# An order of instructions found at build time by a clock per engine, and one transpose for both heads' last keys

## The chip, the cores and the metric

The kernel runs on one core of a Trainium2 chip. The metric is the device time of one execution in microseconds (us). TensorE (PE) multiplies, VectorE (DVE), ScalarE (ACT) and GpSimd (POOL) work elementwise or reduce, SyncE (SP) only issues transfers; each of the five runs its own instructions in the order in which they were issued to it, and waits on semaphores for the others.

## What is computed

Attention with a threshold, a Fourier mixing with a two-layer MLP, and a gated projection, one after the other:

```python
# attention: batch 4, heads 8, seq 576, head_dim 64
scores = scale * np.matmul(q, k.transpose(0, 1, 3, 2))
thresh = np.max(scores, axis=-1, keepdims=True) - tau
scores = np.where(scores >= thresh, scores, -1000000000.0)
attn = np.exp(scores - np.max(scores, axis=-1, keepdims=True))
attn = attn / (np.sum(attn, axis=-1, keepdims=True) + 1e-09)
x = np.matmul(attn, v)                      # then (B, S, H * D)
# Fourier mixing and MLP: d_model 512, hidden 2048
u = x + np.real(np.fft.fft(np.fft.fft(x, axis=1), axis=2))
un = (u - mu) / np.sqrt(var + 1e-06)
y = u + np.maximum(un @ w_ch1, 0.0) @ w_ch2
# gate: a causal convolution of 5 steps over y
out = (1.0 / (1.0 + np.exp(-gate_pre)) * (y @ w_val)) @ w_out
```

The weights arrive as 64-bit floats.

## The kernel before

**Attention** goes over 16 pairs of heads (4 batches of 4 pairs). A pair has 9 tiles: four of 128 queries for each head (h = 0 and 1), and one (h = 2) that holds the last 64 queries of both. For a tile, TensorE makes the scores (L539, two halves of 288 keys on the two halves of the array's rows), VectorE the negated maximum (L551), ScalarE the exponential (L558), VectorE the mask with the row sums (L568). ScalarE adds 1e-9 to the sums (L704), VectorE takes reciprocals (L672), GpSimd scales the tile (L575), and TensorE transposes its first 512 keys in four pieces (L609), which ScalarE copies out (L618). Scores have two PSUM buffers, so a tile's scores wait for the mask two tiles before. The last 64 keys of a head are the "tail": they are transposed apart (L589, 128 queries of one head at a time into 64 rows, on half the array's columns) and copied into th (L594), whose other 64 rows are zero (cleared in lines 172 to 174). Then the probabilities multiply v (L267, the two heads side by side on the two halves of the array's columns), once for the first 256 queries (c = 0) and once for the other 320, and ScalarE copies the result to xt (L270).

**Fourier stages.** A batch's four pairs are folded by GpSimd (L320 to L328) and run through 87 matmuls in two stages (L231), whose result GpSimd adds to x (L425 to L436) and SyncE stores as u_d.

**MLP.** The 2304 rows of u are cut in 5 chunks of 512, 384, 384, 512 and 512. In a chunk each of 16 hidden blocks takes 12 matmuls (h, L1045), a Relu (L1048), a split in high and low part (L1049) and 12 matmuls into four accumulators (c, L1061). **Weights** come as 32 pieces of 512 KB (raw, L852), which VectorE (L99, L100, L103, L104, L105), ScalarE (L101, L102, L108) and GpSimd (L109) turn into high and low float32 parts. The first 16 pieces may be stored in DRAM (e_h, e_l, L905) and reloaded (L835) since room for weights in SBUF opens in steps as attention's pools close: one of 16 blocks after the last keys, 8 when the last pair is folded, all when the last Fourier result is stored ("end" in on_mark, line 1165). Chunk 0's matmuls start when the score buffers are closed, and its last c block waits for "end". Then come the **gate** and the output (L1381, L1399).

**What sets the order.** Attention is a loop over steps of two tiles (line 656). In each step the pieces named in ORDER are issued one after the other:

```python
ORDER = 'R A1 F1 M0 N0 Q T0 M1 E0 E1 T1 U0 H1 TH P1 H3 A2 K0 F2 K1 C S2 S3 H2 WD WD N1 WP U1 WA P2'
```

M0, M1 are the maxima, E the exponentials, K the masks, C the sums, R the reciprocals of the step before, N its scaling, T the transposes of the tiles four behind (LAG), S2 and S3 the scores of the two tiles ahead. P1 and P2 issue tails, multiplications with v and Fourier matmuls from queues, up to a budget of ns (FILLS), and WD, WA, WP one operation each of the weights' conversion. After the last tile the letters of CYCLE do the same for the rest and chunk 0 (act(), line 1205). A transfer is issued where its piece of code stands; nearly all go through SyncE's queue.

## Time and profile before

| | us |
|---|---|
| median of 3 runs (lowest, highest) | 897.75 (897.50, 903.26) |
| the profiled execution, its own time | 897.85 |
| its span, first to last instruction | 896.1 |
| TensorE busy (4902 matmuls) | 837.1 |
| VectorE busy | 554.8 |
| ScalarE busy | 427.0 |
| GpSimd busy | 376.9 |

Busy time is the union of an engine's instructions over the whole span. The ends of matmuls are modelled, so two of them overlap by part of their length, and the distance between two starts says more than a duration. The stages have different limits; the rows further down are read by stretch. One matmul of the program with 32-bit operands shows as two in the profile, except the transposes.

### The profile page before, as it was taken

The numbers are of one execution on the slowest core, as the hardware profiler recorded it, in microseconds if no ns is written. First come the engines' busy times: TensorE is split into PE (matmuls) and PEld (weight loads), VectorE is DVE, ScalarE is ACT, GpSimd is POOL, SyncE is SP. The second block draws the span as 40 slices with busy tenths as digits, with TensorE's granted clock in tenths as the row PEclk, the third lists the DMA queues.
The fourth block names the chain that finished last, engine by engine and source line by source line (L and its number), as shares of the span: only waits on it lengthen the run. The fifth ranks groups of instructions, "written<-read, shape, count | busy, mean of one in ns | idle before, by whom it ended". The sixth has DMA issues, their size and how long they took to land.

```text
span 896.1 us, 13937 instructions
## 1 busy us (share of the span) xinstructions
PE 837.1 (93%) x4902; PEld 660.9 (74%) x4902; DVE 554.8 (62%) x1214; ACT 427.0 (48%) x854; POOL 376.9 (42%) x449
## 2 busy tenths in 40 slices
PE   6897899889997898999879999999999999999998
PEld 4554566546654665688669999999888888898896
DVE  7897987887989877257885443623122565527740
ACT  3776867667768575355453233232122232124432
POOL 3447855684599454443643132222010200056421
PEclk8999999999999899999989999999999999999999
DMA  7458237461592275772794044114000230253111
GB/s 190 118 146 246 67 110 235 141 191 41 166 318 71 71 235 177 245 251 89 255 361 171 18 165 130 71 60 128 2 1 0 101 100 1 99 183 107 60 41 65
DMA packets 63612, 117.10 MB, mean 131 GB/s; under 512 B 12466, under 2 KB 20530, under 8 KB 63544
## 3 DMA queue, kind: packets, MB, share of 16 engines
q1 hardware_dynamic: 56008, 92.36, 32.1%
q0 software_dynamic: 7104, 23.57, 8.1%
q8 instruction: 39, 0.64, 0.3%
q10 hardware_dynamic: 432, 0.30, 0.1%
q14 instruction: 29, 0.24, 0.1%
HBM read 84.73 MB, written 31.47 MB: 130 GB/s over the span
## 4 chain that ended last, share of the span: by engine, by line
PE 72%; DVE 14%; POOL 4%; DMA 4%; issue 3%; ACT 2%; SPq 1%; DVEq 0%; POOLq 0%; ACTq 0%
PE c L1061 20%; PE h L1045 19%; PE s L539 7%; PE f L267 6%; PE v L1381 5%; PE o L1399 5%; PE f L231 5%; PE t L609 4%; DVE p L568 4%; DVE neg L551 3%; POOL p L575 2%; DVE cx L103 1%; DVE raw L104 1%; PE f L589 1%; DMA qt<-in_q 1%
## 5 line engine op out<-in xcount | busy, mean ns | idle before, releaser
L1049 DVE SCALAR_TENSOR_TENSOR hl<-h,hh 128x512 fp32r<-128x512 f32 (+1 forms) x80 | 50.9, 636 | 186.0 <-ACT hh L1048 186.0
L1048 ACT ACTIVATE hh<-h 128x512 fp32r<-128x512 f32 (+1 forms) x80 | 44.3, 553 | 243.4 <-PE h L1045 243.3
L575 POOL TENSOR_SCALAR p<-p,su 128x576 f32<-128x576 f32 x144 | 111.3, 779 | 82.1 <-DVE su L672 74.7
L539 PE MATMUL s<-kt,qt 64*128 64x288 f32 (+1 forms) x640 | 101.2, 446 | 34.1 <-DVE p L568 29.3
L568 DVE SCALAR_TENSOR_TENSOR p<-s,thr,e 128x576 f32<-128x576 f32 x144 | 112.0, 815 | 19.6 <-ACT e L558 13.3
L1061 PE MATMUL c<-hl,w1h 128*128 128x512 f32 (+1 forms) x320 | 118.1, 369 | 0.1
L1061 PE MATMUL c<-hh,w1h 128*128 128x512 f32 (+1 forms) x320 | 118.1, 369 | 0.0
L1061 PE MATMUL c<-hh,w1l 128*128 128x512 f32 (+1 forms) x320 | 118.0, 369 | 0.0
L558 ACT ACTIVATE e<-s,neg 128x576 f32<-128x576 f32 x144 | 100.2, 738 | 36.2 <-DVE neg L551 36.0
L551 DVE TENSOR_REDUCE neg<-s 128x1 f32<-128x576 f32 x144 | 101.6, 746 | 15.7 <-PE s L539 15.6
L539 PEld LDWEIGHTS s<-kt,qt 64*128 64x128 f32 (+1 forms) x640 | 47.6, 179 | 76.2 <-issue 49.8
L609 PEld LDWEIGHTS t<-ident,p 128*128 128x128 f32 x576 | 63.5, 142 | 32.2 <-issue 15.4
L618 ACT ACTIVATE m<-t 128x512 f32<-128x512 f32 x144 | 84.3, 586 | 4.8 <-PE t L609 4.3
L609 PE MATMUL t<-ident,p 128*128 128x128 f32 x576 | 81.0, 282 | 5.4 <-POOL p L575 5.2
L1045 PE MATMUL h<-unh,w0h 128*128 128x512 f32 (+1 forms) x320 | 79.9, 371 | 3.8 <-ACT w0h L108 2.8
L1045 PE MATMUL h<-unh,w0l 128*128 128x512 f32 (+1 forms) x320 | 80.2, 372 | 2.7 <-POOL w0l L109 2.2
L1045 PE MATMUL h<-unl,w0h 128*128 128x512 f32 (+1 forms) x320 | 79.5, 370 | 0.0
L267 PE MATMUL f<-m,v 128*64 128x320 f32 (+1 forms) x512 | 72.5, 413 | 0.0
L1045 PEld LDWEIGHTS h<-unh,w0h 128*128 128x128 f32 x320 | 59.1, 189 | 12.0 <-ACT w0h L108 3.2
L1045 PEld LDWEIGHTS h<-unh,w0l 128*128 128x128 f32 x320 | 59.5, 191 | 11.3 <-POOL w0l L109 2.6
L1061 PEld LDWEIGHTS c<-hl,w1h 128*128 128x128 f32 x320 | 60.4, 189 | 8.5 <-DVE hl L1049 0.8
L1061 PEld LDWEIGHTS c<-hh,w1h 128*128 128x128 f32 x320 | 60.5, 189 | 7.9 <-issue 0.5
(232 smaller groups left out, 1427.0 us busy)
## 6 DMA issues: line engine op xcount, KB each, us to landing
raw<-in_moe_w_ch POOLq DMA_DIRECT2D x32, 512.0 KB, 5.7
qt<-in_q SPq DMA_DIRECT2D x30, 288.0 KB, 5.6
kt<-in_k SPq DMA_DIRECT2D x16, 288.0 KB, 4.8
ypad<-y_d SPq DMA_DIRECT2D x16, 288.0 KB, 3.8
out<-os SPq DMA_DIRECT2D x18, 256.0 KB, 2.0
v<-in_v SPq DMA_DIRECT2D x16, 256.0 KB, 2.7
e_h<-cx SPq DMA_DIRECT2D x16, 256.0 KB, 4.9
e_l<-ct SPq DMA_DIRECT2D x16, 256.0 KB, 3.5
```

Source lines behind the costliest of these rows:

```text
L231: PE.matmul(out=o, lhsT=l, rhs=r, start=(i == 0), stop=(i == n - 1))
L267: PE.matmul(out=f[h * 64:h * 64 + 64, 0:n], lhsT=w, rhs=r, start=(t == 0), stop=(t == 4))
L539: PE.matmul(out=s[o, c, 0:HALF], lhsT=qt[w, hh, q], rhs=kt[w, hh, :], start=True, stop=True)
L551: DVE.tensor_reduce(out=neg[i][:, j, 0:1], in_=sc[g][:, :, 0:HALF], axis=AX.XY, op=ALU.max, negate=True)
L558: ACT.activation(e, sc[g][:, :, 0:HALF], AF.Exp, bias=neg[g // 2][:, g % 2, 0:1], scale=1.0)
L568: DVE.scalar_tensor_tensor(out=p_view(g).rearrange("p (a b) -> p a b", a=2), in0=sc.pop(g)[:, :, 0:HALF], scalar=thr[g // 2][:, j], in1=ex ...
L575: POOL.tensor_scalar(out=v, in0=v, scalar1=su, scalar2=1.0, op0=ALU.mult, op1=ALU.mult)
L609: PE.matmul(out=f[:, t, :], lhsT=pv[:, t * 128:(t + 1) * 128], rhs=ident, is_transpose=True, start=(t == 0), stop=(t == 3))
L618: tq.append(lambda: ACT.activation(o, fv, AF.Copy))
L1045: PE.matmul(out=f[:, 0:n], lhsT=ww[:, k * 128:(k + 1) * 128], rhs=x[:, k, 0:n], start=(i == 0), stop=(i == 3 * KB - 1))
L1049: DVE.scalar_tensor_tensor(out=hl, in0=f[:, 0:n], scalar=0.0, in1=f32(hh), op0=ALU.max, op1=ALU.subtract)
L1061: PE.matmul(out=ch[c][o][:, 0:n], lhsT=ww[:, o * 128:(o + 1) * 128], rhs=x, start=(at_ == 0 and i == 0), stop=(at_ == FB - 1 and i == 2))
```

## The change

ORDER, CYCLE and the loop over steps are replaced by a class Loom. Each tile, tail, multiplication with v, Fourier transform, weight piece and block of chunk 0 is a generator. Before each instruction it yields the engine, an assumed length in ns, a rank and, for TensorE, the array's shape (row, col, full); between them it yields what it comes after. Loom keeps a clock per engine, adds a cost when TensorE's shape changes (SWITCH) and when an operation of VectorE and GpSimd would meet ("port"), and issues next the instruction with the earliest start, low ranks first. The order is fixed at build time; on the chip each engine still runs it in that order. Weight operations have rank 9, below all else, and Fourier matmuls are due one by one over 32 tiles (SPREAD). The convolution weights' conversion, one block of code before, becomes single operations of rank 9.

Beside it, the second head's keys are laid out so that its tail comes first (np.roll). One transpose of 128 x 128 turns both heads' last keys of a row block (L668); th holds head 0 in rows 0 to 63 and head 1 in rows 64 to 127, and vt is zero in the other half. For the 64 last queries two small matmuls do it (L672). kt gets a third copy of 288 columns for this (128x864): the second head's keys in their old order, for the last 64 queries. There are six buffers for probabilities, five before.

The diff, cut:

```diff
-ORDER = 'R A1 F1 M0 N0 Q T0 M1 E0 E1 T1 U0 H1 TH P1 H3 A2 K0 F2 K1 C S2 S3 H2 WD WD N1 WP U1 WA P2'
...
-PBUFS = 5
...
+PBUFS = 6
...
+SPREAD = 32
...
+RANK = {"D": 9, "A": 9, "P": 3}
...
+class Loom:
+    OVER = {"PE": 0.0, "DVE": 88.0, "ACT": 108.0, "POOL": 45.0}
+    SIGNAL = {"PE": 200.0, "DVE": 40.0, "ACT": 40.0, "POOL": 80.0}
+    SWITCH = {"full": 146.0, "row": 188.0, "col": 138.0}
...
+    def cost(self, t, s):
+        e, ns, rank, *how = t.want
+        if e == "PE" and self.shape not in how:
+            ns += self.SWITCH[how[0]]
+        if "port" in how:
+            ns += max(self.port["POOL" if e == "DVE" else "DVE"] - s, 0.0)
+        return ns
...
+    def pick(self, e):
+        c = [(self.start(t), t) for t in self.tasks if t.want[0] == e]
+        c = [x for x in c if x[0] is not None]
+        if not c:
+            return None
+        if e == "PE":
+            return min(c, key=lambda x: (self.score(*x), x[1].seq))
+        first = min(s for s, _ in c)
+        s, t = min((x for x in c if x[0] <= first + NEAR), key=lambda x: (self.rank(x[1]), x[0], x[1].seq))
+        late = s + self.cost(t, s) - HOLD[e]
+        if self.rank(t) >= 1:
+            better = [x for x in c if self.rank(x[1]) < 1 and x[0] < late]
+            if better:
+                s, t = min(better, key=lambda x: (x[0], self.rank(x[1])))
+        return s, t
+
+    def score(self, s, t):
+        r = self.rank(t)
+        v = s + (0.0 if self.shape in t.want else SWAP)
+        return v + 100.0 * r if r < 1 else v + FILL + 300.0 * (r - 1) - (STAY if t is self.last else 0.0)
...
-        ths = [[const.tile([128, 2, n], F32, name=f"th{i}_{n}") for n in (256, 320)] for i in range(2)]
-        for t in [vt for _, vt in vs] + ths[0] + ths[1]:
-            DVE.memset(t[64:128], 0.0)
+        ths = [[const.tile([128, n], F32, name=f"th{i}_{n}") for n in (256, 320)] for i in range(2)]
+        for _, vt in vs:
+            for h in range(2):
+                DVE.memset(vt[64 - h * 64:128 - h * 64, h], 0.0)
...
         def g_prep_qk(p):
+            if p >= 2:
+                yield "after", ("scored", p - 2)
             qt, kt = load_qk(p)
-            for _ in range(WAIT_QK):
-                yield
+            yield "delay", 7500.0
+            yield "POOL", 1060.0, 0.1, "port"
             POOL.tensor_scalar(out=kt, in0=kt, scalar1=alpha[:, 0:1], scalar2=1.0, op0=ALU.mult, op1=ALU.mult)
             kq[p] = (qt, kt)
-
-        def load_v(p):
+            loom.mark("kq", p)
...
             conv_w.load()
-            for _ in range(4):
-                yield
-            conv_w.convert()
-
+            yield "delay", 12000.0
+            for kind, op in conv_w.stages():
+                yield {"D": ("DVE", 170.0, 9), "A": ("ACT", 260.0, 9), "P": ("POOL", 222.0, 9)}[kind]
+                op()
...
+        def due(tile, least=1.0):
+            return lambda: max(2.0 + (tile - len(p_s)) / NPT, 1.0) if tile > len(p_s) else least
...
         def g_fft(b):
...
+            def rank():
+                done[0] += 1
+                r = due(NPT * (b + 1) + FFT_LATE + SPREAD * done[0] / FFT_OPS)
+                return (lambda: min(r(), END)) if b == B - 1 else r
...
-                    PE.matmul(out=s[o, c, 0:HALF], lhsT=qt[w, hh, q], rhs=kt[w, hh, :], start=True, stop=True)
+                    PE.matmul(out=s[o, c, 0:HALF], lhsT=qt[w, hh, q], rhs=kt[w, 2 if h == 2 and hh else hh], start=True, stop=True)
...
+        def g_sum(u):
+            yield "ACT", 203.0, 0.2
+            ACT.activation(ssum[u], ssum[u], AF.Copy, bias=1e-9)
+            yield "DVE", 155.0, 0.0
+            DVE.reciprocal(ssum[u], ssum[u])
+            loom.mark("r", u)
+
+        def g_tail(p, rows):
+            for j, i in enumerate(rows):
+                yield ("PE", 112.0 if i < 4 else 120.0, 0.4, "full" if i < 4 else "col", *(["room"] if j == 0 else []))
+                if j == 0:
+                    f, room = fill_tile()
+                x = p_t[p, i]
+                if i < 4:
+                    PE.transpose(f[:, j * 128:(j + 1) * 128], x[:, MAIN:MAIN + 2 * TAIL], ident)
+                else:
+                    for h in range(2):
+                        w = slice(h * 64, h * 64 + 64)
+                        PE.matmul(out=f[w, 0:64], lhsT=x[:, MAIN:S], rhs=ident[:, w], start=True, stop=True)
+            for i in rows:
+                loom.mark("tailed", p, i)
+            o, n = (256, 64) if rows[0] == 4 else (0, 256)
+            th = ths[p % 2][0 if rows[0] == 0 else 1]
+            yield "ACT", act(n), 0.3
+            ACT.activation(th[:, o:o + n], f[:, 0:n], AF.Copy)
+            loom.free(room)
+            loom.mark("th", p, rows[0])
...
+        def g_tile(g):
...
+            yield "after", ("kq", p), *([("s", g - 1)] if g else []), *([("k", g - 2)] if g > 1 else [])
+            yield "PE", 490.0 if h < 2 else 600.0, 0.1, "row"
+            emit_s(g)
+            loom.mark("s", g)
...
+            yield "DVE", 745.0, 0.3
...
+            yield "after", ("r", u), *([("n", g - 1)] if g else [])
+            yield "POOL", 737.0, 0.1, "port"
...
+            loom.mark("n", g)
+            yield "after", *([("t", g - 1)] if g else [("n", 0)]), *([("mc", g - 2)] if g > 1 else []), *([("pv", p - 2, c)] if p > 1 else [])
+            yield "PE", 437.0, 0.5, "full"
...
-            pv = p_view(g)
+            pv = v[:, TAIL if h == 1 else 0:]
...
-            if h == 1 and i % 2 == 1:
-                q_tail.append(g_tail(p, c, [p_t[p, i - 1 + j][:, hh * S + MAIN:hh * S + S] for hh in range(2) for j in range(2)], th[0:64, :, 0:256], (i - 1, i)))
-            if h == 2:
-                q_tail.append(g_tail(p, c, [p_t[p, i][:, MAIN:S]], th[0:64, :, 256:320], (i,)))
...
-        for u in range(NT // 2 + 3):
...
-            for atom in ORDER.split():
-                env[atom]()
...
+        def g_convert(k, raw, room):
             j, i = pieces[k][1]
-            stay = k >= EARLY and not isinstance(j, str)
-            if stay and j not in w:
-                return False
+            yield "delay", 8000.0
+            yield "when", lambda: at[0] == k and spare["cv"] and (k < EARLY or isinstance(j, str) or j in w)
...
+            took = {"D": iter((415.0, 415.0, 677.0, 679.0, 415.0)), "A": iter((715.0, 621.0, 635.0)), "P": iter((1035.0,))}
+            for kind, op in ops:
+                yield {"D": "DVE", "A": "ACT", "P": "POOL"}[kind], next(took[kind]), RANK[kind], "port"
+                op()
...
+            loom.add(g_load())
+            loom.add(g_first())
+            loom.run(lambda: heads[1] == FB)
...
-                    tick()
-                    slot("DAP", 4)
+                if c in (1, 2):
+                    loom.run(until=loom.now["PE"])
...
-    c["k"] = k.reshape(B, NP, 2, 2, HALF, D).transpose(0, 1, 3, 5, 2, 4).reshape(B, NP, 2 * D, 2, HALF)
+    k = np.stack([k[:, :, 0], np.roll(k[:, :, 1], TAIL, axis=-2), k[:, :, 1]], axis=2)
+    c["k"] = k.reshape(B, NP, 3, 2, HALF, D).transpose(0, 1, 3, 5, 2, 4).reshape(B, NP, 2 * D, 3, HALF)
```

On TensorE, in attention without a Fourier transform near: second half of the second pair, rows of before. s are scores, t transposes into the tile that m is copied from, f<-ident,p tails, f<-m and f<-th the multiplication with v.

```order
L539 MATMUL s<-kt,qt 128x288 x4
L609 MATMUL t<-ident,p 128x128 x8
L589 MATMUL f<-ident,p 64x128 x5
L539 MATMUL s<-kt,qt 128x288 x4
L609 MATMUL t<-ident,p 128x128 x8
L267 MATMUL f<-m_603,v_195 64x320 x8
L539 MATMUL s<-kt,qt 128x288 x4
L267 MATMUL f<-th_320_200,vt_196 64x320 x2
L609 MATMUL t<-ident,p 128x128 x8
L589 MATMUL f<-ident,p 64x128 x4
L539 MATMUL s<-kt,qt 64x288 x4
L539 MATMUL s<-kt,qt 128x288 x2
```

Here the transposes are those of tiles four to five behind the scores just ahead of them, and tails and multiplications with v stand where a budget let them in.

The same place after the change:

```order
L641 MATMUL s<-kt,qt 128x288 x4
L421 MATMUL f<-th_256_199,vt_196 64x256 x2
L739 MATMUL t<-ident,p 128x128 x8
L641 MATMUL s<-kt,qt 64x288 x4
L641 MATMUL s<-kt,qt 128x288 x2
L421 MATMUL f<-m_571,v_195 64x320 x6
L739 MATMUL t<-ident,p 128x128 x8
L668 MATMUL f<-ident,p 128x128 x2
L641 MATMUL s<-kt,qt 128x288 x4
L421 MATMUL f<-m_571,v_195 64x320 x2
L421 MATMUL f<-th_320_200,vt_196 64x320 x2
L739 MATMUL t<-ident,p 128x128 x8
```

A tail is two transposes of 128 rows in place of four of 64; the multiplication with v is cut in pieces (x6, x2) that stand directly behind scores; a step's transposes follow scores that are two tiles nearer than before.

On TensorE again, at the last Fourier transform, which runs beside chunk 0 (h and c are its blocks). Before, the second stage stands in pieces of 18, 9 and 18 matmuls between blocks; the last of them:

```order
L1045 MATMUL h<-unh,w0h_4643 128x512 x4
L1045 MATMUL h<-unh,w0l_4644 128x512 x4
L1045 MATMUL h<-unl,w0h_4643 128x512 x4
L231 MATMUL f<-csh,aeh 128x290 x3
L231 MATMUL f<-csh,ael 128x290 x3
L231 MATMUL f<-csl,aeh 128x290 x3
L231 MATMUL f<-ssh,boh 128x290 x3
L231 MATMUL f<-ssh,bol 128x290 x3
L231 MATMUL f<-ssl,boh 128x290 x3
L1061 MATMUL c_4535<-hh,w1h_4637 128x512
L1061 MATMUL c_4535<-hh,w1l_4638 128x512
```

Each such piece stands between a hidden block and an output block.

After, its 45 matmuls stand in one piece, in the middle of a hidden block:

```order
L1201 MATMUL h<-unh,w0h_4525 128x512 x4
L1201 MATMUL h<-unh,w0l_4526 128x512 x4
L553 MATMUL f<-csh,aeh 2x290 x3
L553 MATMUL f<-csh,ael 2x290 x3
L553 MATMUL f<-csl,aeh 2x290 x3
L553 MATMUL f<-csh,aeh 128x290 x3
L553 MATMUL f<-csh,ael 128x290 x3
L553 MATMUL f<-csl,aeh 128x290 x3
L553 MATMUL f<-ssh,boh 128x290 x3
L553 MATMUL f<-ssh,bol 128x290 x3
L553 MATMUL f<-ssl,boh 128x290 x3
```

Ahead of the last of these matmuls stand 7 c and 9 h blocks of chunk 0 before, and 3 c and 4.7 h blocks after.

## Rows read from the trace of the kernel before

**Rows 1.** Windows: length, busy us (count) of PE, PEld, DVE, ACT, POOL, clock, DMA.

```profile
8.70:351.60 342.90, 304.90 (x2184) 193.18 (x2180) 289.37 (x695) 243.13 (x511) 217.25 (x279) 0.98 0.52 155
351.60:479.10 127.50, 115.25 (x557) 92.62 (x554) 83.38 (x132) 62.75 (x119) 58.62 (x68) 0.96 0.65 226
479.10:896.10 417.00, 412.24 (x2151) 370.92 (x2149) 177.61 (x363) 119.62 (x222) 100.82 (x100) 1.00 0.23 81
```

**Rows 2.** TensorE's waits in stretch A: for whom, total us, times, longest.

```profile
PE s L539 <- DVE p L568: 29.3, 26, 2.5
PE t L609 <- POOL p L575: 3.8, 6, 1.1
```

**Rows 3.** The chain that ended last, stretch A: start, us, what.

```profile
63.26 7.87 DMA qt<-in_q
72.01 4.30 DMA cw_raw<-in_moe_conv_w
...
118.34 2.10 PE f L231 x16
...
195.14 6.81 DMA kt<-in_k
```

**Rows 4.** Timeline: start, us, engine, line, operation, tiles, count [idle before].

```profile
1.35 2.37 DVE L174 MEMSET th<- 64x512 f32 x4
...
4.01 3.35 PE L628 MATMUL idle<-idle 128*128 128x128 f32 x14 [4.01 <-DVE idle L625]
...
350.23 1.40 PE L539 MATMUL s<-kt,qt 64*128 64x288 f32 x12
```

**Rows 5.** Timeline of TensorE, 130 to 144 us.

```profile
130.21 0.63 PE L589 MATMUL f<-ident,p 128*64 128x128 f32 x4
130.67 1.04 PE L609 MATMUL t<-ident,p 128*128 128x128 f32 x8
131.47 0.65 PE L231 MATMUL f<-csh,aeh 97*2 97x290 f32 x3
...
139.37 1.95 PE L267 MATMUL f<-m,v 128*64 128x256 f32 x16
141.25 1.09 PE L609 MATMUL t<-ident,p 128*128 128x128 f32 x8
142.27 0.65 PE L267 MATMUL f<-th,vt 128*64 128x256 f32 x4
...
143.93 1.24 PE L539 MATMUL s<-kt,qt 64*128 64x288 f32 x8
```

**Rows 6.** Groups by line, stretch A: count, busy us, mean ns, idle before.

```profile
L568 DVE SCALAR_TENSOR_TENSOR p<-s,thr,e 128x576 f32<-128x576 f32 x142 | 110.4, 815 | 19.6 <-ACT e L558 13.3
L575 POOL TENSOR_SCALAR p<-p,su 128x576 f32<-128x576 f32 x140 | 108.0, 777 | 75.3 <-DVE su L672 67.8 <-PE t L609 3.0 <-PE s L539 2.5
...
L704 ACT ACTIVATE su<-su 128x2 f32<-128x2 f32 x71 | 14.3, 201 | 20.3 <-DVE p L568 18.9
...
L672 DVE RECIPROCAL su<-su 128x2 f32<-128x2 f32 x71 | 11.4, 161 | 13.1 <-ACT su L704 13.1
```

**Rows 7.** Windows, VectorE's operations on raw alone: length, busy us (count), clock, DMA.

```profile
8.70:351.60 342.90, 48.72 (x80) 0.98 0.52 155
351.60:479.10 127.50, 54.03 (x80) 0.96 0.65 226
```

**Rows 8.** One line, whole run: ns min/median/max, first and last start us.

```profile
L100 DVE TENSOR_SCALAR ct<-raw x40: 407/420/2633, 36.2 to 574.7; 128x512 int32<-128x512 int32 x40
```

**Rows 9.** Windows, all engines, ahead of chunk 0's end.

```profile
425.60:470.50 44.90, 36.35 (x140) 28.90 (x139) 37.91 (x59) 22.95 (x42) 26.39 (x29) 0.89 0.86 307
```

**Rows 10.** The chain that ended last, in stretch B.

```profile
442.43 5.22 DMA w1l<-e_l
...
473.70 5.44 PE c L1061 x24
```

**Rows 11.** Timeline of GpSimd, the last Fourier transform's last sum.

```profile
436.81 0.97 POOL L436 TENSOR_TENSOR xel<-xel,xoh 128x287 f32<-128x287 f32 x1
```

More of the change, by code (lines that the diff above doesn't have):

```diff
@@ L1 @@
 from collections import deque
[L2 removed]
+from contextlib import ExitStack, contextmanager
 from types import SimpleNamespace
@@ L376, in g_fft @@
+                    for i, (xx, dd) in enumerate(ops):
+                        yield ("PE", n / 2.4 + 13.5, rank(), "full", *(["room"] if i == 0 else []))
+                        if i == 0:
+                            f, room = fill_tile()
+                        PE.matmul(out=f[0:m, 0:n], lhsT=xx, rhs=dd, start=(i == 0), stop=(i == len(ops) - 1))
+                    loom.add(g_parts(kind, nb, m, n, f, room))
             fold.pop(b)
-            spent_fold.add(b)
-            yield "sync"
+            loom.mark("spent", b)
@@ L402, in g_fft @@
+            yield ("after", *[("part", b, k, nb) for k in range(2) for nb in range(3)])
+            if b:
+                yield "after", ("added", b - 1, 1)
+            sets = []
             for j in range(2):
+                if j and b < B - 1:
+                    yield "after", ("added", b, 0)
                 x, xr, ws, dd, sm = buffers(j)
@@ L769, in mlp, with stage, go @@
+        def stage(name, then):
+            def go():
+                stacks[name].close()
+                then(name)
+            loom.stages.append((lambda: all(k in loom.done for k in needs[name]), go))
+        yield stage, list(stacks)
+def mlp(tc, right, ps_f, attention, loom, a, u_d, y_d, dram, wide, cw, out):
     nc = tc.nc
@@ new lines, in g_mean @@
+        def g_mean(c, parts, name):
+            n = CHUNKS[c]
+            for i, t in enumerate(parts):
+                yield ("PE", n / 2.4 + 13.5, 1, "full", *([name] if i == 0 else []))
+                if i == 0:
+                    f = ps_f.tile([128, 512], F32, tag="f", name="f") if name == "room" else got["ps_h"].tile([128, 512], F32, tag="h", name="mean")
+                    room = loom.room(name)
+                PE.matmul(out=f[:, 0:n], lhsT=got["ones"], rhs=t, start=(i == 0), stop=(i == 1))
+            return f[:, 0:n], room
@@ L1109, in g_mean @@
-        def g_mean(parts, mu):
-            yield "room"
-            f = hooks["fill_tile"]()[:, 0:CHUNKS[0]]
-            for i, t in enumerate(parts):
-                PE.matmul(out=f, lhsT=got["ones"], rhs=t, start=(i == 0), stop=(i == 1))
-                yield 216.0
-            def first():
-                ACT.activation(mu, f, AF.Copy)
-                started.add(0)
-            hooks["done"](first)
-        def late_var():
-            while 0 not in split or "r" not in got:
-                yield
-            yield from g_var(0, DVE)
-            yield
@@ L1127, in mlp @@
-        seen = set()
-        pre = late_var()
-        tail = None
+            w1h, w1l = w[j][0]
+            i = 0
+            for ww, x in ((w1h, uh), (w1l, uh), (w1h, ul)):
+                yield ("PE", KB * (n / 2.4 + 13.5), 2.2, "full", *(["room_h"] if i == 0 else []))
+                if i == 0:
+                    f = got["ps_h"].tile([128, 512], F32, tag="h", name="h")
+                    room = loom.room("room_h")
+                for k in range(KB):
+                    PE.matmul(out=f[:, 0:n], lhsT=ww[:, k * 128:(k + 1) * 128], rhs=x[:, k, 0:n], start=(i == 0), stop=(i == 3 * KB - 1))
+                    i += 1
```

1111 lines of the change are left out of this document (537 added, 574 removed).

## The prediction

> **What bounds the kernel now.** I read the table of windows first, cut at two places of the program: 351.6 us, where the last score matmul ends [rows 4], and 479.1 us, where MLP chunk 0's last output block ends (473.70 + 5.44 [rows 10]). That gives stretch A (attention, with three Fourier transforms in it), B (the last transform and chunk 0) and C (chunks 1 to 4 and the gate). In C TensorE is busy 412.2 of 417.0 us [rows 1]: it is the bound there, and the change gives it the same matmuls. In A it is busy 304.9 of 342.9 us and VectorE 289.4; in B 115.3 of 127.5 [rows 1]. So up to 38.0 + 12.3 us of TensorE's idle time can be won, plus whatever matmul time goes away, and all of it lies ahead of 479.1 us.
>
> The waits come next. In A the main one is scores waiting for the mask on VectorE, 29.3 us in 26 waits; transposes waiting for GpSimd's normalization cost 3.8 us [rows 2]. The chain of waits shows that some of these are transfers at root: 7.87 us for queries, 4.30 us for the convolution weights, 6.81 us for keys [rows 3]. So two engines that have 84 and 89% of the stretch to do lose the rest to each other and to late transfers. That is what an order can win.
>
> **The change, part by part.** The order shows what moves; times are from rows.
>
> *Start.* Four clearings of th are gone (lines 172 to 174 before): 2.37 us of VectorE ahead of the clearing that the idle matmuls wait for [rows 4]. Those run 4.01 to 7.36 and the first scores stand behind them. The gain is between 0 (keys and queries are late instead) and 2.4; I take **1.0**.
>
> *Tail transposes.* Before, 135 of L589 stand ahead of the last score. Four take 130.67 - 130.21 = 0.46 us [rows 5], 0.115 each, 15.5 us. After, 60 full transposes and 30 small ones stand there. A full one costs what L609 costs ahead of another full-shape matmul: (131.47 - 130.67) / 8 = 0.10 [rows 5], 6.0 us; no row shows the small form, which lies between 0 and 0.115, and I take the upper end since its passes look like L589's: 3.5 us. Gain **6.0** (6.0 to 9.5).
>
> *Changes of shape.* Scores use half the array's rows, the probabilities times v half its columns, the rest all of it. Counted in the order up to the last score, TensorE changes shape 234 times before and 167 after. Eight L609 take 131.47 - 130.67 = 0.80 us to the start of a full-shape matmul and 142.27 - 141.25 = 1.02 to that of a column-shape one [rows 5]: 0.22 for the change. Sixteen L267 take 1.88 up to the L609 behind them [rows 5], which leaves little for a change in that direction, so the price lies between 0.10 and 0.22; I take 0.2, as the nearer rows are those of entering: 67 x 0.2 = **13.4** (6.7 to 14.7). The Trainium skill, TensorEngine Tiling (Array Packing), Key Properties, says that changing the tiling mode drains the engine; the 0.22 us agrees. It gives no figure, and by it alone the sum would stand.
>
> *Moved out of A.* 18 Fourier matmuls (0.131 each, 2.10 / 16 [rows 3]), 12 transposes (0.1) and 8 of L267 (16 instructions, 1.88 [rows 5]) now come behind the last score: 2.4 + 1.2 + 1.9 = 5.5 us less in A, 5.5 more in B.
>
> So TensorE's work in A falls from 304.9 to 304.9 - 6.0 - 13.4 - 5.5 = 280.0 us.
>
> *The other engines in A.* VectorE: 16 weight pieces are converted there before (80 operations, 48.72 us [rows 7], 3.05 a piece) and 13 after, 289.4 - 9.1 = 280.3. The third copy of the keys (kt is 128x864, not 576) makes GpSimd's scaling half as long again, some 0.37 us for each of 15 pairs; it hides in GpSimd's 125.7 us of idle time in A [rows 1]. If a pair's keys were late, it would be on the path, 5.6 us in all.
>
> *Idle time left in A.* It lies between 38.0 (as now) and near 0. Against its end: TensorE and VectorE both have 280 us to do, and the scores, maxima and masks hand to each other in turn. For a real gain: transforms are spread over 32 tiles (rank() in g_fft) where before one batch's 87 matmuls stand within nine steps of two tiles; fillers are placed where an engine would stand idle; the convolution weights are converted one operation at a time, 12 us behind their loads, so the 4.30 us goes. The other two transfers keep their place in the program and their queue, SyncE's, where the stores of converted weights still stand ahead of them. I take **28**. Then A ends at 8.7 + 280.0 + 28 - 1.0 = 315.7 against 351.6, a gain of 35.9.
>
> *Stretch B.* Work rises by 5.5. The last transform's final matmul now has 3 output blocks and 4.7 hidden blocks of chunk 0 ahead of it, where it had 7 and 9: 8.3 blocks of 2.72 us (5.44 / 2 [rows 10]), 22.6 us sooner in chunk 0. What ends the transform, L436 at 437.8 [rows 11], opens the room for the last weights, and behind it stand the 5.22 us transfer of weights [rows 10] and 8.6 us of TensorE's idle time, at a granted clock that fell while TensorE stood still more often (mean 0.89 between its levels of 2.4 and 1.2 GHz) [rows 9]. I take 6.0 of that idle time and 3.0 us of clock as won (0.11 x 36.4 us busy would be 4). Three more pieces are converted in B, 54.03 / 16 = 3.38 us each [rows 7], 10.1 on VectorE, which has 44.1 us of idle time there [rows 1] and 22.6 us more notice; I cost them at nothing. If that cover is gone they stand in front of hidden blocks. B: 5.5 - 6.0 - 3.0 = **-3.5**.
>
> C: 0. **Sum:** -35.9 - 3.5 = -39.4; the profiled execution took 897.85 us (span 896.1 and 1.75 around it), the median is 897.75: **858.5 us**.
>
> **Rivals.** *1. Only the work goes, the idle time stays.* The engines keep standing in each other's way for 38.0 us in A. For it: VectorE has 280 us in a stretch that would be 318 long, so the loop of score, maximum, exponential and mask may simply have that grain. Against it: the three long transfers in the chain are no grain. A gains 24.9 + 1.0 = 25.9, B 0: 872.0 us.
>
> *2. Chunk 0 gives it back.* As 1, and the three pieces moved into B land in front of the blocks that need them (their operations have the lowest rank): 10.1, and the 5.5 of moved matmuls finds no idle time: +15.6, 887.6 us. For it: in B today hidden blocks wait for converted weights, and VectorE is at 83.4 of 127.5 us [rows 1]. Against it: room for late weights opens 22.6 us sooner.
>
> *3. Transposes wait for the normalization (slower).* Before, a tile's transposes are issued with 5 or 6 tiles scored ahead; after, 81 of the first 135 with 4 or fewer. With four, only the score of the tile three ahead (0.62 us, half of 1.24 [rows 5]) stands between the mask and the transpose, and in that time must pass the sum (0.201), the reciprocal (0.161) and the scaling (0.777) [rows 6] with some 0.2 of handing over: 0.7 to 0.75 us short in every step of two tiles, and every score behind it in TensorE's queue is late as well. Over 72 steps that is 54 us, 912.5 us in all; the time passes the old one at 39.4 / 72 = 0.55 us a step. Against it: in 29 of the 70 places other matmuls stand behind the scores, and a step has room, since the next scores wait for two more masks (0.815 us each [rows 6]). For it: conversions on VectorE take up to 2.6 us where the median is 0.42 [rows 8], so an operation placed as a short filler can be long. The Trainium skill, SBUF — State Buffer, Who interferes with whom, says why: VectorE in its two-port mode or with two SBUF operands and GpSimd exclude each other for a whole instruction, and whoever came first blocks the other. The trace agrees as far as the 2.6 us goes. By that rule fillers beside the normalizations would bring about this rival, whose price stands above.
>
> **How the numbers follow.** The forecast 0.57 (its own range 845 to 870, idle time in A from 15 to 38), rival 1 0.17, rival 2 0.14, rival 3 0.12. The time is the forecast's. The range runs from 837 (idle time in A near 12, B at -9) to 892, which holds rivals 1 and 2 and leaves out the third and the far low end. About 1%, 9 us, can be told from no change here. Faster by more: the forecast, rival 1 and the lower part of rival 2, 0.77; within 1%: the rest of rival 2 and a weak rival 3, 0.12; slower 0.11.
>
> **What would show it.** Right: the last score ends near 316 us, TensorE is busy about 280 us up to there with some 28 idle; L651/L706/L723 steps are about 4.2 us apart; no 4.30 us wait for the convolution weights; B lasts about 124 us, with the clock at 1.0 to its end; C stays at 417. Rival 1 shows as 38 idle in A; rival 2 as hidden blocks waiting for w0h or w0l; rival 3 as a wait of transposes (L739) for GpSimd (L731) far above 3.8 us. Wrong from the root would be a C that moves, or a shape change that costs much less than 0.2 us: then A's busy time stays near 293.

## The result, and the profile after

The changed kernel takes 874.21 us (median of 4 runs, 873.57 to 875.20) against 897.62 before: ratio 0.973, 95% interval [0.9694, 0.9765]. It is faster by 23.4 us. The forecast was 858.5, so 15.7 us of the gain did not come; rival 1's 872.0 lies nearer. The profiled execution has a span of 871.9 us, 24.2 less than before.

The same cut as in [rows 1]: A up to the last score, B up to chunk 1's first hidden block, C the rest. Columns: length, busy us (count) of PE, PEld, DVE, ACT, POOL, granted clock, DMA share, GB/s. Windows of the changed kernel:

```profile
8.90:326.46 317.56, 292.13 (x2118) 183.51 (x2119) 280.84 (x679) 232.12 (x502) 213.52 (x271) 0.98 0.54 156
326.46:450.50 124.04, 117.77 (x598) 94.94 (x599) 90.14 (x146) 64.82 (x124) 64.09 (x71) 0.99 0.71 244
450.50:871.90 421.40, 414.42 (x2151) 370.96 (x2149) 182.36 (x366) 122.12 (x227) 107.59 (x103) 1.00 0.24 80
```

A is 25.3 us shorter than in [rows 1] (and begins 0.2 later), B 3.5, and C is 4.4 us **longer**. The last score is at the end of A, at 326.5 where I had put it at 316 (start, us, engine, line, operation):

```profile
6.30 2.29 PE L641 MATMUL s<-kt,qt 64*128 64x288 f32 x8 [1.18 <-DMA qt<-in_q]
325.06 1.40 PE L641 MATMUL s<-kt,qt 64*128 64x288 f32 x12
```

TensorE's waits in A, to set beside [rows 2] (engine, line, for whom: us in total, times, longest). Scores wait 20 us less for masks; transposes wait 8.6 us more, mostly for ScalarE's copy of the transposes two tiles back:

```profile
PE s L641 <- DVE p L723: 9.5, 15, 2.1
PE t L739 <- ACT m L756: 7.0, 15, 0.8
PE t L739 <- POOL p L731: 5.4, 11, 0.8
```

The three long transfers of [rows 3] are no longer in A's part of the chain of waits, whose only transfer is that of the first queries.

What C lost stands at chunk 3's first hidden block. ScalarE (first fence) and TensorE (second) of the changed kernel, timeline:

```profile
582.06 1.28 ACT L1011 ACT_TABLE_LOAD   x1
584.11 0.69 ACT L1011 ACTIVATE nr<-mean,eps 128x512 f32<-128x512 f32 x1 [0.76 <-PE mean L957]
584.81 1.28 ACT L1012 ACT_TABLE_LOAD   x1
586.11 0.63 ACT L1012 ACTIVATE nr<-nr 128x512 f32<-128x512 f32 x1
586.64 2.18 ACT L1028 ACTIVATE unh<-z 128x512 fp32r<-128x512 f32 x4
```

```profile
585.84 0.34 PE L1063 MATMUL c<-hl,w1h 128*128 128x384 f32 x1
587.31 2.06 PE L1047 MATMUL h<-unh,w0h 128*128 128x512 f32 x4 [1.14 <-ACT unh L1028]
...
590.14 2.26 PE L1047 MATMUL h<-unl,w0h 128*128 128x512 f32 x4
592.24 1.09 PE L1047 MATMUL h<-unh,w0h 128*128 128x512 f32 x4
```

Chunk 3's variance (logarithm L1011, exponential L1012, each with a table load of 1.28 us) stands in ScalarE's queue directly ahead of the split L1028 that the hidden block needs. Before, the same two lay ten us ahead of it (timeline of ScalarE, kernel before):

```profile
600.14 0.69 ACT L1011 ACTIVATE nr<-mean,eps 128x512 f32<-128x512 f32 x1 [0.76 <-PE mean L956]
...
610.95 2.19 ACT L1028 ACTIVATE unh<-z 128x512 fp32r<-128x512 f32 x4
```

From 585.84 to 592.24 TensorE does 0.17 us (one output matmul) and 2.72 us (a hidden block) of work in 6.40: 3.5 us are lost. Another 0.7 is lost at 688.7, behind the gate's operations on VectorE.

### The profile page after: what moved, and what is told of

It reads as the page before. It is cut to its first block, busy times and chain, and to the rows that moved or that the text cites. A ratio compares the mean times of both kernels' runs of the same rounds, so it can differ in the third digit from the quotient of the medians.

```text
span 871.9 us, 13881 instructions
## 1 busy us (share of the span) xinstructions
PE 830.0 (95%) x4886; PEld 653.7 (75%) x4886; DVE 556.8 (64%) x1212; ACT 421.0 (48%) x855; POOL 386.3 (44%) x450
## 4 chain that ended last, share of the span: by engine, by line
PE 65%; DVE 12%; issue 9%; ACT 6%; POOL 4%; DMA 3%; SPq 0%; DVEq 0%; ACTq 0%; POOLq 0%
PE c L1063 14%; PE h L1047 14%; PE f L421 6%; PE s L641 6%; PE v L1434 5%; PE o L1452 5%; PE c L1237 4%; PE h L1201 4%; PE t L739 4%; DVE neg L706 4%; DVE p L723 3%; ACT e L712 2%; POOL p L731 2%; ACT m L756 2%; PE f L540 1%
## 5 line engine op out<-in xcount | busy, mean ns | idle before, releaser
L1051 DVE SCALAR_TENSOR_TENSOR hl<-h,hh 128x384 fp32r<-128x384 f32 (+1 forms) x64 | 39.9, 624 | 150.4 <-ACT hh L1050 146.7
L1050 ACT ACTIVATE hh<-h 128x384 fp32r<-128x384 f32 (+1 forms) x64 | 34.8, 544 | 208.4 <-PE h L1047 202.3
L1063 PE MATMUL c<-hl,w1h 128*128 128x384 f32 (+1 forms) x256 | 92.8, 363 | 0.5 <-DVE hl L1051 0.5
L1063 PE MATMUL c<-hh,w1h 128*128 128x384 f32 (+1 forms) x256 | 92.6, 362 | 0.0
L1063 PE MATMUL c<-hh,w1l 128*128 128x384 f32 (+1 forms) x256 | 92.6, 362 | 0.0
L1047 PE MATMUL h<-unh,w0h 128*128 128x384 f32 (+1 forms) x256 | 62.6, 364 | 1.2 <-ACT unh L1028 1.1
L1047 PE MATMUL h<-unl,w0h 128*128 128x384 f32 (+1 forms) x256 | 62.4, 363 | 0.3
L1047 PE MATMUL h<-unh,w0l 128*128 128x384 f32 (+1 forms) x256 | 61.6, 362 | 0.0
L421 PEld LDWEIGHTS f<-m,v 128*64 128x64 f32 x512 | 34.4, 140 | 28.1 <-issue 9.2
L1072 POOL TENSOR_TENSOR res<-ht,res 128x512 f32<-128x512 f32 (+1 forms) x20 | 23.0, 1185 | 68.7 <-DVE ht L1071 68.7
```

The lines of the kernel that those rows point to most:

```text
L421: PE.matmul(out=f[h * 64:h * 64 + 64, 0:n], lhsT=w, rhs=r, start=(t == 0), stop=(t == 4))
L1047: PE.matmul(out=f[:, 0:n], lhsT=ww[:, k * 128:(k + 1) * 128], rhs=x[:, k, 0:n], start=(i == 0), stop=(i == 3 * KB - 1))
L1063: PE.matmul(out=ch[c][o][:, 0:n], lhsT=ww[:, o * 128:(o + 1) * 128], rhs=x, start=(at_ == 0 and i == 0), stop=(at_ == FB - 1 and i == 2))
```

## The experiments

All are the changed kernel with one edit, or with two where that is said; the edits are cut to the lines that matter. The kernels with alternating shapes, with less for TensorE and with both cuts ran once each. The time before was 897.4 to 898.1 us in each group of runs. Ahead of the last score the changed kernel's instructions are the same in three profiles (its own, that without the empty steps and that with them in chunk 1 alone), and A was 317.6, 315.0 and 318.9 us there: differences of A below 4 us say nothing.

### The price of a change of shape

```diff
+ ...
+ for one in (full, row, col):
+     one(64)
+ for one, other in ((full, row), (full, col), (row, col)):
+     for _ in range(16):
+         one(4)
+         other(4)
```

These stand ahead of the first score; full, row and col issue so many matmuls of the shape on a cleared tile.

> Matmuls on a cleared tile are put ahead of the first score (they reach no output): 64 transposes, 64 in scores' shape and 64 in the column shape, each kind in one run, and then each pair of kinds in turns of four and four, 16 times. The whole gets longer by their time, which says nothing; what counts is the price of a change, from the alternating stretches (32 changes each) less the plain runs. My predicted 0.2 us gives 6.4 us per stretch, 0.13 gives 4.2, free changes give 0. If the sum over both directions is well below 0.4 us for every pair, the prediction's price was too high by itself; if it is 0.4, the price was right and TensorE's work grew elsewhere.

Timeline of TensorE: the plain runs (scores L784, column shape L789; each matmul is two instructions), then pieces of the alternating ones:

```profile
17.41 15.79 PE L784 MATMUL s<-idle 64*128 64x288 f32 x128
33.13 14.03 PE L789 MATMUL idle<-idle 128*64 128x256 f32 x128
47.10 0.66 PE L779 MATMUL idle<-ident,idle 128*128 128x128 f32 x4
47.69 1.24 PE L784 MATMUL s<-idle 64*128 64x288 f32 x8
48.86 0.66 PE L779 MATMUL idle<-ident,idle 128*128 128x128 f32 x4
...
75.81 1.08 PE L789 MATMUL idle<-idle 128*64 128x256 f32 x8
76.82 0.66 PE L779 MATMUL idle<-ident,idle 128*128 128x128 f32 x4
...
101.99 1.08 PE L789 MATMUL idle<-idle 128*64 128x256 f32 x8
103.01 1.24 PE L784 MATMUL s<-idle 64*128 64x288 f32 x8
```

Eight score instructions take 8 x 15.72 / 128 = 0.98 us in a run and 48.86 - 47.69 = 1.17 up to another shape: **0.19 us** to leave the row shape. Eight in the column shape take 0.87 and then 1.01 or 1.02, to either other shape: **0.14**. Four transposes take 0.59 up to the next shape; at 0.109 each, the distance of starts at the end of this kernel's own run of 64, that is **0.15**. What is left behind sets the price, not what comes. Over both directions a pair costs 0.34, 0.29 or 0.33 us, below the 0.4 of the prediction, and the mean over the changed kernel's changes is 0.16, a fifth below my 0.2 and above the fitted 0.13. The planner's own table had nearly these numbers (0.188, 0.146 and 0.138 in SWITCH, charged to the shape that comes), and it stood in the diff. The Trainium skill, TensorEngine Tiling (Array Packing), Key Properties, has the drain without a figure; this run gives it one.

### Changes of shape counted as free

```diff
- SWITCH = {"full": 146.0, "row": 188.0, "col": 138.0}
+ SWITCH = {"full": 0.0, "row": 0.0, "col": 0.0}
- SWAP = 400.0
+ SWAP = 0.0
```

> The planner counts changes of shape as free (both numbers at zero): 344 changes up to the last score instead of 166, with 87 Fourier matmuls and 28 of probabilities times v (some 15 us) moved behind it. At 0.2 us a change as I predicted TensorE's busy time up to the last score is 292 + 36 - 15 = 313 us; at 0.13, as the two traces fit, 292 + 23 - 15 = 300; if changes hide in waits, 277. In the first two cases the whole is slower than 874.2 by about 36 or 23 us less what idle time takes up; in the last it is no slower.

939.74 us, ratio 1.0451 [1.042, 1.0482]. Windows, A and B:

```profile
8.90:345.65 336.75, 301.41 (x1976) 166.21 (x1978) 275.55 (x624) 226.06 (x470) 187.64 (x242) 0.93 0.39 112
345.65:516.70 171.05, 149.86 (x741) 110.40 (x741) 125.69 (x198) 83.54 (x158) 88.91 (x101) 0.96 0.67 227
```

A is 19.2 us longer with some 18 us of matmuls fewer in it. The 178 more changes cost 28 us at the prices above, scores wait for masks 9 us longer (18.6), and two matmuls of a mean (L1113), which this order has in A, wait 10 us. The granted clock is 0.93 there instead of 0.98; what that cost was not taken apart. The larger part of the loss is B, 47 us longer: the transforms pushed out of A stand there, and chunk 0 behind them. An order that ignores these changes loses 65 us, more than the whole change gained.

### The tails alone

```diff
- PE.transpose(f[:, j * 128:(j + 1) * 128], x[:, MAIN:MAIN + 2 * TAIL], ident)
+ for h in range(2):
+     w = slice(h * 64, h * 64 + 64)
+     PE.matmul(out=f[w, j * 128:(j + 1) * 128], lhsT=x[:, MAIN + h * TAIL:MAIN + h * TAIL + TAIL], rhs=ident, ...)
```

> Only the transposes of last keys are put back to one per head (column shape, two of 64 keys in place of one of 128), in an order that the planner finds for them: 182 changes of shape up to the last score instead of 166. Theory: they cost TensorE time like any other work: 60 full ones of 0.104 become 120 small ones of 0.085 to 0.115 (+4 to +7.5 us) and 16 more changes cost 2 to 3: the stretch up to the last score gets 6 to 10 us longer and the time is 880 to 884. Rival: TensorE's 25 us of idle time there take them up: less than 2 us longer, 876 at most.

879.40 us, ratio 0.9787 [0.9757, 0.9817], 5.2 us more than the changed kernel. Window of A:

```profile
8.90:337.71 328.81, 300.78 (x2327) 191.53 (x2329) 287.10 (x685) 236.27 (x510) 214.49 (x271) 0.99 0.54 158
```

A is 11.3 us longer, B 4.0 shorter (120.0). 2.2 of the 11.3 are 20 transposes that this order has ahead of the last score; the other 9 lie in the expected 6 to 10. Idle time did not take them up, and the order without the shared tails still beats the kernel before by 18 us. This form is not that of the kernel before: it has the column shape and pays the changes, which L589's transposes did not, as is shown further down.

### What A's remaining waits hang on

Four edits. Weights loaded later (less for VectorE in A):

```diff
- yield "after", ("k", 1)
+ yield "after", ("s", 100)
```

> The weights' loads begin behind score tile 100 instead of at the first masks: 18 of VectorE's conversion operations stand ahead of the last mask instead of 67, some 30 us of its work less in stretch A; TensorE has there what it had, 12 transposes and 7 changes of shape more (2.5 us). Theory 1, A is bound by TensorE's work with a fixed rest of short waits: A stays between 315 and 322 us (317.5 now) and the whole gets slower, by the up to 30 us of conversions that then stand in front of chunk 0's hidden blocks. Theory 2, VectorE's loop of maximum and mask bounds A and conversions push it: A falls to 300 us or less.

Less for TensorE:

```diff
- for t in range(5):
+ for t in (0, 3, 4):
```

> Leaves out two of the five matmul pairs of the probabilities times v (the output is not the reference's): 116 matmuls less ahead of the last score, 28 us of TensorE's time, against which stand 17 changes of shape (2.8) and 12 transposes (1.3) more. Theory 1, A is bound by TensorE's work with a fixed rest of short waits: A falls from 317.5 to about 294 us. Theory 2, VectorE's loop bounds A (it is busy 281 us there): A stays above 307 us and TensorE's idle time grows instead.

Both together:

```diff
- yield "after", ("k", 1)
+ yield "after", ("s", 100)
  ...
- for t in range(5):
+ for t in (0, 3, 4):
```

> Both earlier cuts together: two of the five matmul pairs of the probabilities times v left out (the output is not the reference's; 24 us net less for TensorE) and the weights' loads behind score tile 100 (21 us less for VectorE in A). The first alone took 14.4 us from A, the second 3.4. Theory: in A TensorE and VectorE are both near their limit, so that each cut alone runs into the other engine; both together give the whole 24 us or more: A 293 or less. Rival: the rest is a fixed chain of hand-overs between score, maximum, exponential and mask, which neither engine's load moves: A stays at 300 or above.

The last two leave out a part of the product, so their output is not the reference's. Windows of A in the three, in this order:

```profile
8.90:323.14 314.24, 291.53 (x2131) 183.51 (x2131) 259.83 (x630) 222.91 (x486) 191.88 (x249) 1.00 0.45 130
```

```profile
8.90:312.07 303.17, 272.33 (x1898) 167.58 (x1899) 269.04 (x656) 230.35 (x496) 201.70 (x259) 0.99 0.52 148
```

```profile
8.90:310.29 301.39, 271.15 (x1898) 168.03 (x1899) 250.86 (x616) 220.74 (x480) 184.51 (x243) 0.99 0.43 121
```

21 us less on VectorE leave A where it was (-3.3, with 2 us more of transposes and changes in it); the whole takes 907.88 us, ratio 1.0127 [1.0098, 1.0156], since B grows by 35.5. So VectorE's load is not A's bound. 24 us less on TensorE take only 14.4 from A, half way between the two theories. Where the rest went shows in TensorE's waits in this second kernel:

```profile
PE t L739 <- POOL p L731: 16.2, 31, 2.1
PE s L641 <- DVE p L723: 8.9, 17, 2.1
```

Scores wait for masks as before the edit, but transposes wait 16.2 us for GpSimd's normalization instead of 5.4. Both cuts together take 16.2 from A: easing VectorE adds 1.8, which says nothing, and A stays 1.4 us above the 300 of the third run's rival, a chain of hand-overs that neither engine's load moves. 301.4 us are 72 steps of 4.19. Two such steps in the third kernel (its timeline):

```profile
199.87 1.24 PE L641 MATMUL s<-kt,qt 64*128 64x288 f32 x8
200.81 1.41 DVE L706 TENSOR_REDUCE neg<-s 128x1 f32<-128x576 f32 x2
201.65 1.41 ACT L712 ACTIVATE e<-s,neg 128x576 f32<-128x576 f32 x2 [1.22 <-DVE neg L706]
202.54 0.82 DVE L723 SCALAR_TENSOR_TENSOR p<-s,thr,e 128x576 f32<-128x576 f32 x1
203.28 0.81 DVE L723 SCALAR_TENSOR_TENSOR p<-s,thr,e 128x576 f32<-128x576 f32 x1
204.44 1.24 PE L641 MATMUL s<-kt,qt 64*128 64x288 f32 x8
...
208.00 1.50 PE L641 MATMUL s<-kt,qt 64*128 64x288 f32 x8
```

Two scores, their maxima, exponentials and masks, and 4.57 us on the next two scores, which need the room (two score tiles) that the masks free. But 3.56 us later the next scores start, and in this kernel's A the distance from a score to that of two tiles on is 3.45 us at its shortest and below 4.2 in 93 of 142 places. So 4.19 is a mean and not the length of the ring; the ring alone would allow some 248 us (72 x 3.45). TensorE's waits in the third kernel are 12.2 us for masks and 10.9 for normalizations. What keeps A near 300 was not shown. The changed kernel needs 4.41 us a step (317.6 / 72), before it was 4.76.

The third edit makes transposes wait for five more tiles to be scored:

```diff
- yield "after", *([("t", g - 1)] if g else [("n", 0)]), ...
+ yield "after", *([("t", g - 1)] if g else [("n", 0)]), ..., ("s", min(g + 5, NT - 1))
```

> A tile's transposes are issued only with five more tiles scored, which undoes the shorter lag that my rival 3 was about; 173 changes of shape instead of 166 (1.1 us). Theory: the shorter lag costs little, since a step has room for the normalization: transposes' wait for GpSimd (5.4 us in all) goes, A changes by -5 to +2 us, the whole is 869 to 877. Rival 3's mechanism, hidden in many short waits: A falls by 10 us or more, the whole to 864 or less.

878.08 us, ratio 0.9767 [0.9733, 0.9802]; A is 321.7. TensorE's waits in A, the longest:

```profile
PE s L641 <- DVE p L723: 23.0, 45, 2.1
```

The waits of transposes go, as expected (those for GpSimd are no longer listed, those for ScalarE's copy fall to 1.7), but scores now wait 23.0 us instead of 9.5. The sum stays: the wait only changes its place. A went up by 4.2 and the whole by 3.9, a little above what I expected. So in the changed kernel's A rival 3's mechanism was not hidden; with TensorE's load cut it begins to show, by the 16.2 us above.

The fourth lets a Fourier transform come in a bunch:

```diff
- SPREAD = 32
+ SPREAD = 6
```

> A Fourier transform is due within 6 tiles instead of 32; 18 Fourier matmuls and 28 transposes more stand ahead of the last score, 10 of the probabilities times v less (some 4 us of work in all); 165 changes of shape, as now. My prediction held the spreading to win idle time: then A gets longer by those 4 us and by 5 to 10 of waits, 327 to 332, and the whole by 5 to 10 us. Rival: the order has room for a bunched transform as well: A 321 to 322, the whole within 2 us of 874.2.

869.36 us, ratio 0.9685 [0.9663, 0.9708], 4.9 **less** than the changed kernel. Windows, A and B:

```profile
8.90:327.51 318.61, 292.88 (x2149) 186.33 (x2149) 282.49 (x684) 237.73 (x513) 214.27 (x272) 1.00 0.56 161
327.51:446.13 118.62, 112.82 (x570) 90.87 (x570) 88.42 (x142) 60.14 (x114) 66.14 (x72) 0.99 0.70 242
```

A is as long as before this edit with 4 us more work in it, and B has that work less. Spreading the transforms, on which I had rested part of the idle time's fall, won nothing.

### The planner's rule on VectorE and GpSimd

The word is taken from every request that holds it; one of them:

```diff
- yield "POOL", 737.0, 0.1, "port"
+ yield "POOL", 737.0, 0.1
  ...
```

> The planner no longer counts VectorE and GpSimd as excluding each other (the word port is taken from all its requests); 165 changes of shape, 12 transposes more in A (1.3 us). Theory: that rule does little for the order, as the normalization lasted 777 ns on the mean before the change and 785 after: A within 3 us of 318.8, the whole 872 to 878. Rival, by the Trainium skill's exclusive lock: conversions land on normalizations more often, their mean rises above 850 ns, and A gets longer by 8 us or more.

892.58 us, ratio 0.9943 [0.9924, 0.9962]: 18.4 us lost, and neither expectation named it. Normalizations by line, A:

```profile
L731 POOL TENSOR_SCALAR p<-p,su 128x576 f32<-128x576 f32 x139 | 112.2, 817 | 88.6 <-DVE su L658 77.4 <-PE s L641 5.6 <-PE f L668 2.9
```

Their mean rises to 817 ns from 785, and transposes wait for them 12.1 us instead of 5.4, so the direction is that of the exclusive lock in the Trainium skill, SBUF — State Buffer, Who interferes with whom. But A is only 7.0 us longer (324.5). B is 10.5 us longer (134.5), with 5.7 us of it a mean's matmul waiting for its sums (L1101). Which placement in B the missing rule spoils was not taken apart.

### The empty steps, and a faster kernel

The change put two empty steps ahead of the variance matmul of chunks 1 to 4. Taken out everywhere:

```diff
  parts = hi_lo(sq[2])
- yield
- yield
  var = col_mean(parts)
```

> The two empty steps ahead of a later chunk's variance matmul (in g_var) are taken out, all else as in the changed kernel. Theory: they are what stretch C lost, since chunk 3's logarithm and exponential, with two table loads of 1.28 us, came to stand in ScalarE's queue directly ahead of the split that chunk 3's first hidden block needs. Then TensorE does not stand still between 585.8 and 592, chunks 1 to 4 take 311 us as before the change instead of 315, and the time falls from 874.2 to about 870.3. Rival: chunk 3 starts late because of where the planner puts the late weight conversions in chunks 1 and 2: then the stall stays and the time is within 1 us of 874.2.

876.62 us, ratio 0.9755 [0.9728, 0.9782]: not faster. The stall at chunk 3 is gone, but C is 423.4. Timeline of TensorE in chunk 1, and VectorE's at the same place:

```profile
464.78 0.44 PE L957 MATMUL mean<-cs,ones 128*128 128x384 f32 x1 [1.05 <-ACT cs L946]
466.88 0.58 PE L957 MATMUL mean<-cs,ones 128*128 128x384 f32 x1 [1.66 <-DVE cs L947]
467.25 1.48 PE L1045 MATMUL h<-unh,w0h 128*128 128x384 f32 x4
```

```profile
465.07 0.68 DVE L255 SCALAR_TENSOR_TENSOR cx<-raw,cx 128x512 int32<-128x512 int32 x1
...
466.27 0.55 DVE L947 TENSOR_TENSOR cs<-cs 128x384 fp32r<-128x384 f32 x1
```

Without the steps chunk 1's variance matmul waits in TensorE's queue for a low part (L947) that stands behind weight conversions, and the hidden block behind it runs at near half pace: between 465 and 470 us the mean granted clock is 0.70. From the output matmul at 463.38 to that at 470.80 TensorE has 2.6 us of work in 7.4: 4.8 us go there. So the steps do earn something in chunk 1 and cost 3.5 us in chunk 3. Kept in chunk 1 alone:

```diff
+ if c == 1:
      yield
      yield
```

> The two empty steps ahead of the variance matmul stay in chunk 1 alone, where without them TensorE waited for sums that VectorE made between weight conversions (about 5 us), and go in chunks 2 to 4, where they put the logarithm's table loads in front of chunk 3's split (3.5 us). Theory: both losses are gone, chunks 1 to 4 take 311 to 312 us and the time is 870 to 871.5. Rival: the place of the later normalizations hangs on chunk 1's as well, so that chunk 3's first hidden block still waits: 874.

871.75 us (870.34 to 875.98), ratio 0.9719 [0.9695, 0.9743]. The medians lie 2.5 us apart and the ranges overlap, so the rows decide: C is 419.9, TensorE no longer waits at chunk 3's start, and chunk 2's variance now waits instead (0.99 + 0.29 us at 522). With the steps in chunks 1 and 2 (if c < 3), and SPREAD 6:

> Two edits of the changed kernel: Fourier transforms due within 6 tiles (which alone gave A 318.6 and B 118.6 us), and the empty steps ahead of the variance matmul kept in chunks 1 and 2 and taken out in 3 and 4. Theory: A 318.6, B 118.6, C falls from 421 to about 418 as neither chunk 2's variance nor chunk 3's split is waited for: 864 to 866 us. Rival: chunk 3's variance needs chunk 2's steps gone as well, so the 3.5 us at chunk 3's first hidden block stay: 868 to 870.

866.39 us (865.22 to 867.40), ratio 0.9652 [0.9629, 0.9676]: the fastest of all, 7.8 us under the changed kernel. Both waits are gone, but C is 420.8, not 418. The gate in the last chunk now holds VectorE longer (timelines of VectorE and TensorE):

```profile
679.12 0.52 DVE L1389 TENSOR_SCALAR gate<-ypad,cw 128x576 f32<-128x576 f32 x1 [1.63 <-DMA ypad<-y_d]
679.55 1.54 DVE L1391 SCALAR_TENSOR_TENSOR gate<-ypad,cw,gate 128x576 f32<-128x576 f32 x2
681.01 0.68 DVE L1052 SCALAR_TENSOR_TENSOR hl<-h,hh 128x512 fp32r<-128x512 f32 x1
```

```profile
681.75 0.74 PE L1064 MATMUL c<-hl,w1h 128*128 128x512 f32 x1 [1.88 <-DVE hl L1052]
```

An operation of the gate waits for a transfer, and hl, which TensorE needs, stands behind it.

## Why the prediction was right in its direction and too high in its size

**Start (-1.0).** Right: the first scores begin at 6.30 us where they began at 7.30.

**Work in A (-24.9: tails 6.0, changes 13.4, moved 5.5).** This is the step that failed: the changes of shape were priced too high. Among the 234 changes of before I had counted L589's transposes as column shape, since they fill half the array's columns. Beside full transposes they pay nothing. Timeline of TensorE, kernel before:

```profile
160.53 1.04 PE L609 MATMUL t<-ident,p 128*128 128x128 f32 x8
161.40 0.27 PE L589 MATMUL f<-ident,p 128*64 128x128 f32 x1
```

Eight L609 take 0.87 us up to an L589, 0.109 each, as in a run; of 28 places without a wait where an L589 stands behind an L609, 27 have that distance, and the six of the other direction have 0.109 to 0.137. Up to a multiplication with v the eight take 1.02 [rows 5]: 0.15 for that change. I had read 0.22, since I set the 1.02 against 0.80 up to a Fourier matmul; but a Fourier matmul starts 0.03 us after the last transpose ahead of it, so the 0.80 is too short. With L589 as full shape and the measured prices, taken by the shape that is left, 208 changes before are 69 x 0.19 + 85 x 0.15 + 54 x 0.14 = 33.4 us and 167 after are 69 x 0.19 + 56 x 0.15 + 42 x 0.14 = 27.4: **6.0** instead of 13.4. The order could not save the dearest ones, since each pair of scores must still be left once. Tails: 135 L589 at 0.109 are 14.7 us, and after them stand 60 full ones at 0.109 and 30 small ones at 0.083 (the changed kernel's trace has nine places in A where two of them take 0.17 us up to the next matmul), 9.0, which makes 5.7. Moved work is 5.6 by the counts. Sum 17.3.

**Idle time in A (38 to 28).** Right in its direction. The last score ends 25.1 us sooner: 1.0 by the start, 17.3 by work, so some 7 by waits, where I had 10; A varies by up to 4 between equal orders, so the difference of 3 cannot be told from none. What won the 7 was not shown. The three long transfers left the chain, but spreading the transforms, one of my reasons, won nothing. How I measured idle time was wrong all the same. [Rows 1] give TensorE 304.9 us busy of 342.9, and I took the difference for the waits. Busy time of TensorE holds modelled ends, which cover the start of a wait. The transposes by line, before and after, show it:

```profile
L609 PE MATMUL t<-ident,p 128*128 128x128 f32 x552 | 77.6, 282 | 3.9 <-POOL p L575 3.8
```

```profile
L739 PE MATMUL t<-ident,p 128*128 128x128 f32 x541 | 85.2, 286 | 13.4 <-ACT m L756 7.0 <-POOL p L731 5.4
```

Eleven fewer count as 7.6 us more, because they now come in fours with gaps between them instead of in eights. So busy time fell by 12.8 us where the work fell by 17.3, and the 25.4 us of idle time after are not a fall of 12.6. The Trainium skill, Perfetto Trace Analysis, Tensor Engine Instruction, says that this engine's end times are computed and not observed; the two rows agree, and I should have weighed it.

Two signs that I had called wrong from the root came: a shape change much cheaper than 0.2 us (41 changes that cost 6.0 us, spread over the 67 that I counted, are 0.09 each), with A's busy time near 293 (292.1), and a C that moved. That the busy time lies so near is partly luck, since it holds some of the waits.

**Rival 1** came within 2.2 us with its 872.0 by luck. I gave it 0.17. It let the work fall by 24.9 us, the waits by nothing and C alone; the work fell by 17.3, the waits by some 7, and C lost 4.4. Its mechanism, VectorE's load, did not hold: 21 us less of it won nothing. I had written steps of 4.2 us into the signs to look for and got 4.41.

**Stretch B (-3.5).** Right in each term: 124.0 us (124 forecast), 6.3 us idle where it was 12.3, a clock of 0.99, and conversions that cost nothing. Rival 2 did not come: the only long wait of a hidden block is 4.3 us for the first weights.

**C (0).** Wrong by 4.4 us. I had the same matmuls there and looked no further; the diff's two empty steps stood in it. They move chunk 2's and chunk 3's variance two steps each, and ScalarE's order decides the rest, as the run without them shows by the stall's absence. But no run brought C back to 417: at best it was 419.9, as other waits came where the stall had been.

**Rival 3** did not come: transposes wait 5.4 us for GpSimd in all, where it needed 0.55 us in each of 72 steps. The longer lag removed that wait and gave it back at the scores. The 2.6 us conversion of [rows 8], which spoke for this rival, starts at 455 us and thus in B; in A of the kernel before the longest was 1.5.

In sum: forecast -35.9 up to the last score (1.0 start, 24.9 work, 10.0 waits), -3.5 in B, 0 in C; found -25.1 (1.0 start, 17.3 work, some 7 waits), -3.5 and +4.4. Of the 15 us missing, 7.6 are work (7.4 of it the price of the changes), 3 are waits that stayed and 4.4 stretch C, 3.5 of it the stall that the empty steps made.

## What to carry over

Compare TensorE's work before and after by counts times start-to-start prices, not by busy time: where groups get shorter, the busy time hides waits. Price a change by the very pair of instructions between which it stands, ahead of counting it: 26 of the 234 here were free, and the trace of before shows it. When a loop of engines hands work in a ring, easing one engine moves the wait to another place; look for it there, and take no mean step for the ring's shortest. And an empty step in a schedule is an edit like any other: it costs nothing where it stands and can put something slow ahead of something urgent two chunks later.

## What the runs showed of the hardware

- Leaving TensorE's row shape cost 0.19 us, the full shape 0.15, the column shape 0.14, whatever came next. Transposes that fill 64 columns (L589) and full ones (L609) followed each other at 0.109 us, as in a run.
- In the kernel with the alternating shapes the first of the run of 64 transposes began 0.213 us apart (27 distances), and from 13.3 us on 0.109 (36 distances). The trace's first record of the granted clock begins at 13.27 us, with 1.00 (2.4 GHz); ahead of it there is none, and the 1.00 that the table of windows gives there stands for no record. TensorE had done 14 idle matmuls and stood still for 1.88 us before the run.
- After TensorE's waits in chunk 1 (1.05 and 1.66 us), the granted clock fell to a mean of 0.70 between 465 and 470 us, between its levels of 2.4 and 1.2 GHz. The hidden block behind took 3.55 us there (467.25 to 470.80) and 2.08 in the changed kernel: 1.5 us on top of the waits.
